# Cutting the last 512 bytes of two cache loads into many small transfers

## The chip, the cores and the metric

The kernel runs on one core of one Trainium2 chip. The core has a matrix engine (TensorE, PE in the profile), a vector engine (VectorE, DVE), a scalar engine (ScalarE, ACT), a general engine (GpSimd, POOL), a queue processor (SyncE, SP) and 16 DMA engines that move data from HBM into the on-chip memory SBUF. The metric is the device time of one execution in microseconds; before the change it is 354.47 us, the median of two executions (354.26 and 354.67).

## The reference, cut to what matters

A decode step for one token of width 512. The large inputs are the two caches: 8 key/value heads, 32768 positions each, 128 numbers of bfloat16 per position, so 8 MiB per head for K and as much for V.

```python
mod = (_silu(c) @ w_mod).reshape(c.shape[0], 6, 1, -1)      # six rows of 512
h = _layernorm(x) * (1 + ca) + sa
q = (h @ wq)                                                # 32 query heads, 4 to a key/value head
scores = einsum('bhqd,bhkd->bhqk', q, k) * Dh ** (-0.5)     # k repeated 4 times
o = einsum('bhqk,bhkd->bhqd', softmax(scores), v)
x = x + ga * (o @ wo)
h = _layernorm(x) * (1 + cb) + sb
x = x + gb * (relu(h @ w1) @ w2)                            # hidden width 1792
```

Every byte of K, V and of the weights is read once and used for a few products only.

## The kernel before, in words

**Tiles.** A head's K (or V) lies in SBUF as 128 partitions with 256 consecutive positions each: 64 KiB in a partition. `kv` and `vv` (L66, L67) are these views of the caches. Three buffers of that size make up the ring (L80); each holds in turn one head's K, one head's V, the pair of `w_mod` and `wq`, or at the end the tail (`wo`, `w1`, `w2`). A new load takes the buffer that was given out three loads earlier, so its transfer is issued only after the work on that earlier content is done.

**Order of loads.** `stream` (L162 to L168) lists the loads by hand: half of K of head 0, `w_mod`, `wq`, the other half of K of head 0, then K of head 1, V of head 0, K of head 2, V of head 1, and so on; the last heads go in halves and quarters, and `wo`, `w1`, `w2` come last. `need` (L171) runs `load` for the next entries of the list until the wanted one is there. `stream_dma` (L153, the transfer itself L154) issues each on SP's queue and stamps it so that the order is kept. A whole head (8 MiB) is one transfer of 128 rows of 64 KiB; a half is 128 rows of 32 KiB. After V of head 0, 14 SP drains follow (L145).

**Completion semaphores.** The framework gives each transfer of SP's and ACT's queues one of eight completion semaphores, in turn. The two small loads of `c` and `A_x` on ACT's queue (L182) take part in the turn. A wait for a transfer is a wait on its semaphore.

**The two loads of the change.** The second half of K of head 0 (the key `UNEVEN`, L57) is cut in `load` (L136 to L141): first all 128 rows without their last 512 bytes (`EDGE`), then the last 512 bytes of rows 0 to 110 (`MOST` is 111), then those of the other 17 rows. V of head 1 is one transfer on SP's queue (L143).

**Compute.** For each head, DVE transposes K in place in eight pieces (L439, 32-bit blocks), PE makes the scores into PSUM (L458), and a softmax over DVE, PE and ACT (L466 to L510) gives the weights, which DVE transposes (L500); PE multiplies them with V (L520) in a loop on PE (L527). Within the loop over heads (L643), K of head g+1 is handled first, then V of head g. K of head 0 is used in quarters: the third transpose and scores of its second half come before the fourth, and only the fourth touches the last 512 bytes. GpSimd does constants in the first 3 us and one memset near the end (L718). After the last head come `wo`, a layer norm, `w1`, `w2` (L784) and the output (L789 to L792).

Of the kernel before, what the change touches and what calls it, by code (L numbers as in the profile page):

```python
# [17 lines left out]
def kernel(  # L18
# [14 lines left out]
    nc = tc.nc  # L33
    P = 128
    _, _, D = A_x.shape
    _, Hkv, Sk, Dh = A_k_cache.shape
# [6 lines left out]
    TK = 64  # L43
# [10 lines left out]

    OUT0, OUT1 = 30, 34

    UNEVEN, EDGE, MOST = ("k", 0, (2, 3)), 2 * TK * Dh - D // 2, 111  # L57
    SPACE = 14
    assert Dh == 128 and REP == 4 and D == 512 and FT == W2P[-1][1] and NTILE == 4
    scale = float(Dh) ** -0.5  # L60
    eps = 1e-5
# [8 lines left out]
    def wo_v(i):  # L70
        g0, n = WOP[i]
        return A_wo[g0 * REP * Dh:(g0 + n) * REP * Dh, :].rearrange("(p r) d -> p r d", p=P)
# [32 lines left out]
    def piece(name, at, n):  # L105

        if name not in pieces:
            pieces[name] = ring.tile([P, NTILE * TK * Dh], BF16, tag="slot", name=name)
        return pieces[name][:, at:at + n]

    def load(key):
        kind = key[0]
        if kind == "wm":
            t = piece("wmq_sb", 0, WM).rearrange("p (kt n) -> p kt n", kt=KT)
            src = wm_v
        elif kind == "wq":
            t = piece("wmq_sb", WM, WQ).rearrange("p (kt n) -> p kt n", kt=KT)
            src = wq_v
        elif kind in "kv":
            g, steps = key[1], key[2]  # L120
            src = (kv if kind == "k" else vv)[g, :, TK * steps[0]:TK * (steps[-1] + 1), :]
            name = f"Ksb{g}" if kind == "k" else f"Vsb{g}"
            t = piece(name, TK * Dh * steps[0], TK * Dh * len(steps)).rearrange("p (j d) -> p j d", d=Dh)
        elif kind == "wo":
            g0, n = WOP[key[1]]
            t = piece("tail_sb", g0 * REP * D, n * REP * D).rearrange("p (r d) -> p r d", d=D)
            src = wo_v(key[1])
        elif kind == "w1":
            k0, k1 = W1P[key[1]]
            t = piece("tail_sb", WO + k0 * Dff, (k1 - k0) * Dff).rearrange("p (kt f) -> p kt f", f=Dff)  # L130
            src = w1_v[:, k0:k1]
        else:
            f0, f1 = W2P[key[1]]
            t = piece("tail_sb", WO + KT * Dff + f0 * D, (f1 - f0) * D).rearrange("p (f d) -> p f d", d=D)
            src = w2_v[:, f0:f1]
        if key == UNEVEN:  # L136
            row, src_row = (x.rearrange("p j d -> p (j d)") for x in (t, src))
            for rows, cols in (
                (slice(0, P), slice(0, EDGE)), (slice(0, MOST), slice(EDGE, None)), (slice(MOST, P), slice(EDGE, None)),
            ):  # L140
                stream_dma(row[rows, cols], src_row[rows, cols])  # L141
        else:
            stream_dma(t, src)  # L143
        if key[:2] == ("v", 0):
            for _ in range(SPACE):  # L145
                nc.sync.drain()
        if kind in "kv":
            for i, u in enumerate(steps):
                loaded[(kind, g, u)] = t[:, TK * i:TK * (i + 1), :]
        else:  # L150
            loaded[key] = t

    def stream_dma(dst, src):  # L153
        i = nc.sync.dma_start(out=dst, in_=src)  # L154
        tc.stamp_issue_order_token(i.ins, "sp_stream")
        if last_loop:

            tc.add_manual_dep(i.ins, last_loop[0], mybir.DependencyInfo(
                mybir.DependencyClass.NoSync, mybir.DependencyReason.DATA))
# [11 lines left out]
    def need(key):  # L171
        while key not in loaded:
            load(stream[pos[0]])
            pos[0] += 1
        return loaded[key]
# [19 lines left out]
    for hp in range(4):  # L195
        h, par = hp // 2, hp % 2
        src = AP(ib.tensor, ib.offset + 64 * h + par, [[ib.ap[0][0], P], [0, 4], [2, 32]])
# [8 lines left out]
        out=mask4, in_=ident_f[:].rearrange("p (x q) -> p q x", q=REP), op=ALU.add, axis=AX.X,  # L206
# [3 lines left out]
    for n in sorted({n * REP for _, n in WOP}):  # L210
        cmask[n] = const.tile([P, P // n], F32, name=f"cmask{n}")
        nc.vector.tensor_reduce(
            out=cmask[n][:], in_=ident_f[:].rearrange("p (c r) -> p c r", r=n), op=ALU.add, axis=AX.X,
# [3 lines left out]
            out=rsel_f[:], in_=ident_f[:].rearrange("p (c r) -> p r c", r=n), op=ALU.add, axis=AX.X,  # L217
# [6 lines left out]
        out=smask[:], in_=ident_f[0:16, 0:16].rearrange("p (s q) -> p s q", q=REP), op=ALU.add, axis=AX.X,  # L224
# [8 lines left out]
        out=place32[:], in_=ident_f[:].rearrange("p (j m) -> p m j", m=32), op=ALU.add, axis=AX.X,  # L233
# [4 lines left out]
        out=rowpick[:, OUT0:OUT1], in_=ident_f[:].rearrange("p (j m) -> p j m", m=32), op=ALU.add, axis=AX.X,  # L238
# [8 lines left out]
        out=cx_bd, in0=cx_row[:].unsqueeze(1).to_broadcast([16, 8, D // 8]),  # L247
# [80 lines left out]
    for u in range(2):  # L328
        for half in range(2):
            t = need(("k", 0, u))[:, 32 * half:32 * half + 32, :].rearrange("p j d -> p (j d)").bitcast(F32)  # L330
# [29 lines left out]
    def four_rows(e, name):  # L360
# [16 lines left out]
        out=nca[:], in0=modT_sb[:, KT:2 * KT], scalar1=-1.0, scalar2=-1.0, op0=ALU.mult, op1=ALU.add,  # L377
# [3 lines left out]
        out=ncb[:], in0=modT_sb[:, 4 * KT:5 * KT], scalar1=-1.0, scalar2=-1.0, op0=ALU.mult, op1=ALU.add,  # L381
# [17 lines left out]
    for i in range(2):  # L399
        nc.vector.transpose(out=q_cols[:, i, :], in_=q_ps[i])  # L400
        nc.scalar.copy(
            out=qT_sb[:, 16 * i:16 * (i + 1)], in_=q_cols[:, i, :].rearrange("p (h r) -> p h r", r=32)[:, :, 0],
# [230 lines left out]
    with tc.manual_schedule(engines={mybir.EngineType.PE, mybir.EngineType.DVE}):  # L633
# [54 lines left out]
        for u in (2, 3):  # L688
# [49 lines left out]
            out=x1T[:], in0=x1T[:], scalar=1.0, in1=xT, op0=ALU.mult, op1=ALU.add, accum_out=stat2[:, 0:1],  # L738
# [31 lines left out]
        for f0, f1 in ((0, FT // 2), (FT // 2, FT)):  # L770
            nc.vector.transpose(out=hidT[:, f0:f1], in_=hid_v[:, f0:f1])
            nc.scalar.activation(
                out=AP(hb.tensor, hb.offset + 32 * f0 + 31, [hb.ap[0], [32, f1 - f0]]),
                in_=hidT[:, f0:f1, 0], func=ACT.Relu,
            )

        for part, (f0, f1) in enumerate(W2P):
            w2_sb = need(("w2", part))
            for ft in range(f0, f1):
                for i in (0, 2, 1, 3):  # L780
                    row = OUT0 + i
                    to, w = (0, 32) if row < 32 else (32, OUT1 - 32)
                    at = 32 * ft + 31 - (row - to)
# [39 lines left out]
```

## Time and profile before

| What | Value |
|---|---|
| Median of two executions | 354.47 us |
| The profiled execution: span from first to last instruction | 352.6 us |
| Bytes read from HBM in it | 149.42 MB, 424 GB/s over the span |
| PE, DVE, ACT, POOL busy | 79%, 57%, 7%, 1% of the span |
| DMA share of SP's queue | 98.5% of 16 engines' span |

The profiled execution has no time of its own on record beside its span. The timed executions are 1.9 us longer than that span at the median; the profile does not say what that difference is made of.

How to read it: the page lists the busy time of each engine, the span in 40 slices, the DMA queues (q1 is SP's, q10 ACT's), the chain of work that ended last and the costliest groups. "Us to landing" of a transfer counts from its issue to the arrival of its last bytes, so it holds the time that it stood in the queue behind earlier ones. In the timeline of SP, a row gives start and duration of an issue, not of the transfer.

### The profile page before, as it was taken

To read this page: it belongs to the slowest core of one execution; us is meant where nothing else is said; L and a number is where in the kernel's file an instruction comes from. 1 tells how busy PE (TensorE), PEld (TensorE's weight loads), DVE (VectorE), ACT (ScalarE), POOL (GpSimd) and SP (SyncE) were. 2 spreads that over 40 slices of the span, in tenths; PEclk is the share of its full clock that TensorE was granted. 3 is DMA by queue.
4 is the path that set the end of the run, shared out by engine and by line. 5 is a ranking of instruction groups with operands and counts; after the bars stand their busy time and mean duration, and the time that the engine had idled before them with its cause. 6 is when DMAs were issued, how large, how long until landed. Compare 5 with 4: busy or idle time off the path is not lost. (4 is left out here: it accounts for less than half of the span.)

```text
span 352.6 us, 3715 instructions
## 1 busy us (share of the span) xinstructions
PE 277.9 (79%) x1310; PEld 113.5 (32%) x1310; DVE 201.0 (57%) x226; ACT 25.1 (7%) x69; POOL 3.1 (1%) x15
## 2 busy tenths in 40 slices
PE   0065891895998599976998499968999799989994
PEld 0021330331333234322333134323444233434442
DVE  6663564984079614974099506975684257744142
ACT  1200103002000200001000200011000100011000
POOL 2000000000000000000000000000000000000000
PEclk9999897798999879998999879996999989999999
DMA  9999989999999999999999999999999999999995
GB/s 357 398 435 452 472 388 461 454 394 454 461 394 448 439 424 439 424 433 439 416 446 446 409 440 461 411 394 454 431 414 435 457 417 420 444 439 409 425 425 214
DMA packets 5224, 149.59 MB, mean 424 GB/s; under 512 B 604, under 2 KB 988, under 8 KB 1628
## 3 DMA queue, kind: packets, MB, share of 16 engines
q1 hardware_dynamic: 5180, 149.43, 98.5%
q8 instruction: 8, 0.13, 0.1%
q14 instruction: 4, 0.03, 0.0%
q10 hardware_dynamic: 32, 0.00, 0.0%
HBM read 149.42 MB, written 0.00 MB: 424 GB/s over the span
## 5 line engine op out<-in xcount | busy, mean ns | idle before, releaser
L439 DVE STREAM_TRANSPOSE Ksb<-Ksb 128x2048 f32<-128x2048 f32 x60 | 133.1, 2276 | 60.2 <-DMA Ksb<-in_A_k_cache_dram 60.2
L520 PE MATMUL o_ps<-Vsb,P_g 128*16 (+1 forms) x512 | 127.0, 408 | 13.0 <-ACT P_g L495 10.0
L458 PE MATMUL S_ps<-Ksb,qbd 128*128 128x512 bf16 x512 | 120.4, 386 | 10.9 <-DVE Ksb L439 9.3
L458 PEld LDWEIGHTS <-qbd 128*128 128x128 bf16 x512 | 49.6, 98 | 78.1 <-issue 21.8
L520 PEld LDWEIGHTS o_ps<-Vsb,P_g 128*16 x352 | 34.0, 97 | 67.8 <-issue 36.5
L520 PEld LDWEIGHTS <-P_g 128*16 128x16 bf16 x160 | 13.8, 90 | 19.0 <-issue 0.4
L420 ACT COPY qbd<-qrep_sb 32x16 bf16<-32x16 bf16 x32 | 6.4, 201 | 175.2 <-PE S_ps L458 174.1
L500 DVE STREAM_TRANSPOSE P_g<-P_g 128x1024 bf16<-128x1024 bf16 x8 | 10.0, 1245 | 14.1 <-ACT P_g L495 14.1
L471 DVE TENSOR_REDUCE m_p<-S_ps 128x1 f32<-128x1024 f32 x7 | 8.6, 1223 | 13.3 <-PE S_ps L458 13.3
L322 PE MATMUL mod_ps<-wmq_sb,siluT 128*1 128x512 bf16 x24 | 3.6, 624 | 9.9 <-DMA wmq_sb<-in_w_mod_dram 9.9
L331 DVE STREAM_TRANSPOSE Ksb<-Ksb 128x2048 f32<-128x2048 f32 x4 | 8.9, 2280 | 1.6 <-DMA Ksb<-in_A_k_cache_dram 1.6
L476 PE MATMUL mT_ps<-ident_f,m_p 128*1 128x128 f32 x8 | 2.2, 270 | 8.9 <-DVE m_p L471 7.9
L495 ACT ACTIVATE P_g<-S_ps,nbias 128x1024 bf16<-128x1024 f32 x8 | 8.9, 1114 | 0.2
L506 PE MATMUL L_ps<-Lexp,ones_f 128*128 128x4 f32 x16 | 3.1, 263 | 6.3 <-DVE Lexp L503 4.3
L492 ACT ACTIVATE nbias<-Mb_ps 128x1 f32<-128x1 f32 x8 | 1.4, 171 | 88.3 <-PE Mb_ps L490 88.3
L509 DVE RECIPROCAL Linv<-L_ps 128x4 f32<-128x4 f32 x8 | 1.3, 164 | 10.9 <-PE L_ps L506 10.9
L252 PE MATMUL xc_ps<-cx_sel,wmq_sb 16*128 16x2 bf16 x4 | 0.3, 172 | 8.7 <-DVE wmq_sb L246 8.7
L555 PE MATMUL acc_ps<-mask_sb,Y 16*128 16x4 f32 x16 | 3.0, 258 | 4.9 <-DVE Y L551 4.9
L548 DVE TENSOR_TENSOR o_ps<-o_ps,smask 16x512 f32<-16x512 f32 x8 | 5.3, 668 | 2.8 <-PE o_ps L520 2.8
L586 DVE CAST o_sb<-o_ps 128x4 bf16<-128x4 f32 (+2 forms) x4 | 0.7, 165 | 10.3 <-PE o_ps L582 10.3
L506 PEld LDWEIGHTS L_ps<-Lexp,ones_f 128*128 128x128 f32 x16 | 2.6, 203 | 9.6 <-issue 5.6
L551 DVE TENSOR_REDUCE Y<-o_ps 16x128 f32<-16x512 f32 x8 | 5.4, 678 | 0.3
(116 smaller groups left out, 82.8 us busy)
## 6 DMA issues: line engine op xcount, KB each, us to landing
Ksb<-in_A_k_cache_dram SPq DMA_DIRECT2D x5, 4096.0 KB, 23.5
Vsb<-in_A_v_cache_dram SPq DMA_DIRECT2D x5, 4096.0 KB, 38.0
wmq_sb<-in_A_wq_dram SPq DMA_DIRECT2D x1, 4096.0 KB, 28.0
Vsb<-in_A_v_cache_dram SPq DMA_DIRECT2D x2, 2048.0 KB, 38.1
Ksb<-in_A_k_cache_dram SPq DMA_DIRECT2D x1, 4032.0 KB, 37.1
wmq_sb<-in_w_mod_dram SPq DMA_DIRECT2D x1, 3072.0 KB, 18.8
tail_sb<-in_A_wo_dram SPq DMA_DIRECT2D x1, 2048.0 KB, 23.0
tail_sb<-in_B_w_dram SPq DMA_DIRECT2D x1, 1792.0 KB, 30.4
```

The lines of the kernel that those rows point to most:

```text
L322: nc.tensor.matmul(dst[j // 4][32 * (j % 4):32 * (j % 4) + 1, :], lhsT=src_T[:, kt:kt + 1], rhs=w[:, kt, j * 512:(j + 1) * 512], start=(kt ...
L331: nc.vector.transpose(out=t, in_=t)
L420: nc.scalar.copy(out=o, in_=i)
L439: t = nc.vector.transpose(out=KTt.bitcast(F32), in_=KTt.bitcast(F32))
L458: nc.tensor.matmul(S_ps_tiles[g], lhsT=qbd[g % 2][:, hp, 4 * (7 - s):4 * (7 - s) + P], rhs=KTv[:, 16 * sl:16 * sl + 16, h, :, par], start= ...
L471: behind_loop(nc.vector.reduce_max(out=m_p[:], in_=S_g.rearrange("p g f -> p (g f)"), axis=AX.X))
L495: nc.scalar.activation(out=P_g[:], in_=S_g.rearrange("p g f -> p (g f)"), func=ACT.Exp, bias=nbias[:], scale=scale, accum_out=l_g[:],)
L500: behind_loop(nc.vector.transpose(out=P_g[:], in_=P_g[:]))
L506: nc.tensor.matmul(L_ps[:], lhsT=ones_f[:], rhs=Lexp[:], start=True, stop=True)
L520: nc.tensor.matmul(o_tiles[g][:], lhsT=PT, rhs=Vx, start=False, stop=False, skip_group_check=True)
L548: nc.vector.tensor_tensor(out=o, in0=o, in1=smask[:].unsqueeze(2).to_broadcast([16, 4, Dh]), op=ALU.mult,)
L551: nc.vector.tensor_reduce(out=Y[:], in_=o.rearrange("p s d -> p d s"), op=ALU.add, axis=AX.X)
```

## The change

Two loads are cut in another way; the bytes and their places in SBUF stay the same.

For the second half of K of head 0, the last 512 bytes of the 128 rows go in 15 transfers in place of two: of 15, 14, 13 and so on down to 2 rows, and one of 9 rows, all on SP's queue behind the transfer of the other columns.

V of head 1 is cut too: SP's transfer leaves out the last 512 bytes of each row, and 16 transfers issued by GpSimd bring these: 14 of 17 rows by 256 bytes, then two of 9 rows by 256 bytes.

```diff
-    UNEVEN, EDGE, MOST = ("k", 0, (2, 3)), 2 * TK * Dh - D // 2, 111
+    UNEVEN, EDGE = ("k", 0, (2, 3)), 2 * TK * Dh - D // 2
     SPACE = 14
+    PROBED = ("v", 1, (0, 1, 2, 3))
...
         if key == UNEVEN:
             row, src_row = (x.rearrange("p j d -> p (j d)") for x in (t, src))
-            for rows, cols in (
-                (slice(0, P), slice(0, EDGE)), (slice(0, MOST), slice(EDGE, None)), (slice(MOST, P), slice(EDGE, None)),
-            ):
-                stream_dma(row[rows, cols], src_row[rows, cols])
+            stream_dma(row[:, 0:EDGE], src_row[:, 0:EDGE])
+            at = 0
+            for n in (15, 14, 13, 12, 11, 10, 9, 8, 7, 6, 5, 4, 3, 2, 9):
+                stream_dma(row[at:at + n, EDGE:], src_row[at:at + n, EDGE:])
+                at += n
+        elif key == PROBED:
+            row, src_row = (x.rearrange("p j d -> p (j d)") for x in (t, src))
+            n = row.shape[1]
+            stream_dma(row[:, 0:n - 256], src_row[:, 0:n - 256])
+            for part in range(7):
+                for c0 in (n - 256, n - 128):
+                    rows, cols = slice(17 * part, 17 * part + 17), slice(c0, c0 + 128)
+                    nc.gpsimd.dma_start(out=row[rows, cols], in_=src_row[rows, cols])
+            for c0 in (n - 256, n - 128):
+                rows, cols = slice(119, P), slice(c0, c0 + 128)
+                nc.gpsimd.dma_start(out=row[rows, cols], in_=src_row[rows, cols])
         else:
             stream_dma(t, src)
```

## The prediction

> **What bounds the kernel now.** I read the page's DMA part first, then the chain.
>
> ```profile
> span 352.6 us, 3715 instructions
> ...
> PE 277.9 (79%) x1310; PEld 113.5 (32%) x1310; DVE 201.0 (57%) x226; ACT 25.1 (7%) x69; POOL 3.1 (1%) x15
> ...
> DMA  9999989999999999999999999999999999999995
> q1 hardware_dynamic: 5180, 149.43, 98.5%
> q8 instruction: 8, 0.13, 0.1%
> HBM read 149.42 MB, written 0.00 MB: 424 GB/s over the span
> ...
> 349.62 0.29 PE end_ps L784 x4
> ```
>
> The reader is to see that the DMA engines are busy in every slice but the last, and that SP's queue alone takes 98.5% of them: 347.3 of 352.6 us, with the rest at the two ends. The last line is from the chain in order of time: the last product runs at 349.62, right behind the last piece of `w2`, and 3.0 us of compute and output end the span. So the time is the length of one unbroken stream of transfers plus fixed ends. A microsecond in which the engines have nothing to move in the middle of the stream is a microsecond of the result; PE (79%) and DVE (57%) cannot take it back. What I look for in the change is therefore whether it makes the stream shorter, or lets it run dry.
>
> **What lets SP issue a transfer.** Next come SP's timeline and the time to landing of single issues, at the end of the kernel, where SP waits for no buffer:
>
> ```profile
> 290.81 0.43 SPq L154 DMA_DIRECT2D Vsb<-in_A_v_cache_dram  x1
> Vsb<-in_A_v_cache_dram SPq DMA_DIRECT2D x1, 2048.0 KB, 40.3
> 313.02 0.33 SPq L154 DMA_DIRECT2D tail_sb<-in_A_wo_dram  x1
> tail_sb<-in_A_wo_dram SPq DMA_DIRECT2D x1, 2048.0 KB, 23.0
> ...
> 331.14 0.33 SPq L154 DMA_DIRECT2D tail_sb<-in_B_w_dram  x1
> 335.99 0.33 SPq L154 DMA_DIRECT2D tail_sb<-in_B_w_dram  x1
> ```
>
> The last quarter of V, issued at 290.81, lands 40.3 us later, at 331.1; the third piece of `w2` is issued at 331.14. The first piece of `wo` lands at 313.02 + 23.0 = 336.0; the fourth piece of `w2` goes at 335.99. Counted in the list of loads, each pair is eight transfers apart (V's last quarter, `wo` four times, `w1`, then `w2` one, two, three). None of these pieces needs the other's data or buffer. They share a semaphore: eight serve all of SP's and ACT's transfers in turn, so **a transfer is issued only when the one eight places before it has landed**. In the old order this never bites ahead of the tail, since few transfers are on their way; I take it as the rule that decides here.
>
> **The change, part by part.** First the K half. The issues at the start, and their landings:
>
> ```profile
> 2.12 0.49 SPq L154 DMA_DIRECT2D Ksb<-in_A_k_cache_dram  x1
> Ksb<-in_A_k_cache_dram SPq DMA_DIRECT2D x1, 4032.0 KB, 37.1
> 8.66 14.46 SPq L154 DMA_DIRECT2D Ksb<-in_A_k_cache_dram  x1
> 313.02 1.75 SPq L154 DMA_DIRECT2D tail_sb<-in_A_wo_dram  x4
> 314.81 0.43 SPq L154 DMA_DIRECT2D tail_sb<-in_B_w_dram  x1
> ```
>
> The large part of the K half is issued at 2.12 and lands at 2.12 + 37.1 = 39.2. In the old kernel two small issues follow, and K of head 1 is handed to the queue from 8.66 to 23.1, long before 39.2: the engines go from one to the other without a pause.
>
> Now 15 small transfers stand between. Number them by rows: the large part, 15, 14, 13, 12, 11, 10, 9 rows fill eight places. The transfer of 8 rows is eight places behind the large part, so SP holds it until 39.2. Behind it in SP's order wait those of 7, 6, 5, 4, 3, 2 and 9 rows and K of head 1, which the engines would need at that very moment; at 39.2 they hold only seven transfers of at most 15 rows. At SP's rate, four issues from 313.02 to 314.81, 0.45 us each, K of head 1 is eight issues after 39.2: 39.2 + 8 x 0.45 = **42.8**. K of head 1 also has to wait for its own forerunner, the transfer of 8 rows, which has had 3.6 us by then; the seven others find theirs long landed. V of head 0 follows at 43.3 and is no problem.
>
> From issue to data there is a start-up, read off the start of the kernel:
>
> ```profile
> 0.74 0.38 SPq L154 DMA_DIRECT2D Ksb<-in_A_k_cache_dram  x1
> Ksb<-in_A_k_cache_dram SPq DMA_DIRECT2D x1, 4096.0 KB, 12.0
> wmq_sb<-in_w_mod_dram SPq DMA_DIRECT2D x1, 3072.0 KB, 18.8
> 1.17 0.43 SPq L154 DMA_DIRECT2D wmq_sb<-in_w_mod_dram  x1
> ...
> 60.18 2.31 DVE L439 STREAM_TRANSPOSE Ksb<-Ksb 128x2048 f32<-128x2048 f32 x1 [0.62 <-DMA Ksb<-in_A_k_cache_dram]
> ```
>
> `w_mod`, queued behind the first K half, lands at 20.0, 7.2 us after that half (12.7) for 3.15 MB: 437 GB/s. At this rate the first half's 4.19 MB are 9.6 us, but 12.0 passed: a start from an empty queue costs 2.4 us, landing included. So K of head 1 (8.39 MB, 19.2 us) lands at 42.8 + 2.4 + 19.2 = 64.4. Unbroken from 39.2 it would land at 58.4: **6.0 us** is the upper end of the loss. In the old kernel it landed only at 60.2, when DVE stops waiting for it: some engines were late there, by the small packets among others. Against that, the loss is **4.2 us**, the lower end, if all of that lateness is gone for good. The lateness at the end of the span has more sources than the first 60 us (instruction loads are on the same engines, 8 packets on q8), so I take most of the upper end: **5.5 us**. The later stream is only shifted: every buffer is freed later by as much as its data came later.
>
> The last 512 bytes of the K half now land with the transfer of 9 rows, issued at 42.3, thus about 44. Only the fourth transpose needs them, and it starts at 39.25 + 3 x 2.2 = 45.9:
>
> ```profile
> 39.25 8.89 DVE L439 STREAM_TRANSPOSE Ksb<-Ksb 128x2048 f32<-128x2048 f32 x4 [3.89 <-DMA Ksb<-in_A_k_cache_dram]
> ```
>
> That is nothing lost, with 2 us of cover; without cover PE's scores of head 0 would wait, on an engine with slack.
>
> What the smaller cuts give the engines: the old 128 rows of 512 bytes sat on few of them.
>
> ```profile
> DMA packets 154, 0.79 MB, mean 524 GB/s; under 512 B 15, under 2 KB 143, under 8 KB 143
> ```
>
> In 38.7 to 40.2 there are 143 - 15 = 128 packets of that size, all of them, so the fullest engine was held for 1.5 us at most; what of that comes back is inside the two ends above. [...]
>
> Then V of head 1. SP's transfer loses 64 KB of 8 MB, under 0.2 us. GpSimd's 16 transfers start when V's buffer is free, as SP's does, and nothing else waits on GpSimd until 313. There is no transfer from GpSimd in the trace. The nearest row is a 1 KB load from ACT's queue beside a full SP queue:
>
> ```profile
> 1.35 0.28 ACTq L182 DMA_DIRECT2D cx_row<-in_A_x_dram  x1
> 7.99 0.68 DVE L246 TENSOR_TENSOR wmq_sb<-cx_row,pick 16x512 bf16<-16x512 bf16 x1 [1.82 <-DMA cx_row<-in_A_x_dram]
> ...
> 79.83 0.33 SPq L154 DMA_DIRECT2D Vsb<-in_A_v_cache_dram  x1
> 123.78 15.57 PE L520 MATMUL o_ps<-Vsb,P_g 128*16 x61 [1.99 <-ACT P_g L495]
> 140.16 0.33 SPq L154 DMA_DIRECT2D Ksb<-in_A_k_cache_dram  x1
> 313.05 0.47 POOL L718 MEMSET tail_sb<- 128x450 bf16 x1 [309.91 <-PE S_ps L458]
> ...
> Vsb<-in_A_v_cache_dram SPq DMA_DIRECT2D x1, 38.2
> 118.48 0.33 SPq L154 DMA_DIRECT2D Vsb<-in_A_v_cache_dram  x1
> ```
>
> It took 6.6 us for one row on each of eight engines, where an engine's 32 KB row is 9.6/8 = 1.2 us: about five rows of the other queue went first. Beside 64 KB rows that is 13 us. If they go eight at a time as on SP's queue, twice over makes 26 us: from 79.8 + 5 to 111, and PE wants V of head 1 at 123.8 + 5. So I price this part at **0**, with nothing below: data that came earlier would gain nothing, since PE waits for ACT's softmax there. If it is late, there is more cover: the next load into this buffer is issued at 140.16, and the queue holds work until V of head 2 lands at 118.48 + 38.2 = 156.7, some 14 us after it counting the start-up.
>
> **Sum:** 5.5 us on a span of 352.6 is 358.1; the timed median, 1.9 us above the span, goes to **360.0**. Two per cent, 7.1 us, is about what a measurement of this kernel can tell from no change, and the forecast lies inside it.
>
> **Rivals.** *The stream does not run dry* (chance 0.08). It needs that SP gets K of head 1 out before 39.2 all the same, because the turn of semaphores runs otherwise than the two pairs above show. Then the old small packets' 1.5 us on the fullest engine is what is left of the change, and a lateness carried to the end is worth all or nothing: 353.0 to 354.5. This is the side of not slower.
>
> *GpSimd's rows come too late* (0.10). If each of its 256-byte rows takes its own turn behind a 64 KB row (2.4 us), 17 rows beside the five turns are 22 turns, 53 us; two rounds are 106 us, V is complete at 191, 62 us after PE wants it, of which 14 are covered: about 48 us more, some 408. With one round, or with several rows to a turn, it is inside the cover. The one-row load does not tell. [...]
>
> *The restart is dearer* (0.10): the first issues after a wait at 0.6 us rather than 0.45, or one engine hit twice by late loads, adds 1.5 to 3.5 us: 361.5 to 363.5, mostly over 2%.
>
> **How the numbers follow.** The forecast has 0.72, from 358.7 (4.2) to 360.5 (6.0), a little wider for the rates. Leaving out the first two rivals (0.18) gives the range 357.5 to 363.5. Slower by over 2%, above 361.6: 0.10 of GpSimd, 0.08 of the dear restart, 0.02 of the forecast's own edge, 0.20. Faster by over 2%: 0.01. Within: 0.79.
>
> **What would show it.** In the changed profile: SP idle ahead of L154 until 39.2, ended by the K half's DMA; eight issues in a row after it; a hole of 4 to 5 us in the DMA busy share from 39.3; K of head 1 landing at 64 in place of 60.2, and every later issue 4 to 6 us later. PE's first product with V of head 1 should wait for ACT, as before, and not for a DMA. It would be wrong if K of head 1 is issued before 39, if the hole is there and the end moves by less than 4 us (an engine that is late anyway), or if GpSimd's transfers land after 129.

## The result, and the profile after

The changed kernel takes 383.08 us (median of two executions, 382.50 and 383.66) against 354.47: the ratio is 1.081, with a 95% interval from 1.0767 to 1.0854. That is 28.6 us slower, far outside the range of 357.5 to 363.5. Single executions of some kernels below, the kernel before among them, are up to 22 us longer than the shortest of the same kernel; the ratios leave out those that are more than 1.5% above the shortest.

The page of the changed kernel, with the lines that answer to those read of before:

```profile
span 381.9 us, 3795 instructions
...
DMA  8999699999999999703999999999999999999991
GB/s 330 439 439 432 228 440 439 439 439 440 432 432 432 420 372 440 330 0 110 434 439 439 432 419 406 414 426 432 439 439 427 432 439 426 414 439 426 418 423 68
...
q1 hardware_dynamic: 5304, 149.36, 91.5%
...
q0 software_dynamic: 512, 0.07, 0.1%
...
HBM read 149.42 MB, written 0.00 MB: 391 GB/s over the span
...
PE 13%; DVE 2%; issue 0%; ACT 0%; ACTq 0%
```

Each slice is 9.5 us wide. The stream now has two holes: a short one in the fifth slice (228 GB/s), which the prediction foresaw, and a deep one from the 17th to the 19th (330, 0 and 110 GB/s), which it did not. SP's queue holds the engines for 91.5% of the span in place of 98.5%. A new queue is there, GpSimd's q0, with 512 packets and next to no bytes. And the chain that ended last is now one of PE. In the kernel before, the same line of the page reads:

```profile
DMA 19%; PE 5%; DVE 3%; SPq 0%; issue 0%
```

The view follows the chain back over the last 60 us or so of the changed kernel, and no DMA is in that part.

SP's timeline shows both holes as late issues:

```profile
2.13 40.17 SPq L167 DMA_DIRECT2D Ksb<-in_A_k_cache_dram  x17
42.42 0.35 SPq L167 DMA_DIRECT2D Vsb<-in_A_v_cache_dram  x1
...
83.98 0.33 SPq L167 DMA_DIRECT2D Vsb<-in_A_v_cache_dram  x1
...
178.82 0.33 SPq L167 DMA_DIRECT2D Ksb<-in_A_k_cache_dram  x1
...
344.55 1.75 SPq L167 DMA_DIRECT2D tail_sb<-in_A_wo_dram  x4
...
379.62 0.29 SPq L805 DMA_DIRECT2D out_dram<-o_bf  x1
```

The first row holds the large part of the K half, the 15 small transfers and K of head 1, and ends at 42.30. V of head 1 goes out at 83.98, 4.15 us later than before (79.83). K of head 4 goes out at 178.82, 38.7 us later (140.16). Then the lateness shrinks: 31.5 us at `wo` (344.55 against 313.02), 29.05 us at the output (before: 350.57).

The two holes by windows, first the changed kernel, then the kernel before; the last two columns are the DMA share and GB/s:

```profile
39.00:44.00 5.00, 5.00 (x21) 2.06 (x20) 4.65 (x3) 0.00 (x0) 0.00 (x0) 0.84 0.62 215
84.00:161.00 77.00, 33.59 (x136) 12.97 (x136) 35.27 (x29) 4.35 (x14) 8.23 (x16) 0.75 0.99 422
161.00:181.00 20.00, 18.11 (x75) 7.28 (x76) 1.61 (x2) 0.00 (x0) 0.00 (x0) 0.85 0.16 52
```

```profile
39.00:44.00 5.00, 5.00 (x23) 2.12 (x22) 4.75 (x3) 0.00 (x0) 0.00 (x0) 0.94 0.99 420
```

From 84 to 161 the stream runs at 422 GB/s, against 424 over the whole span before: GpSimd's transfers hardly slow it here. The hole comes after them, from 161 to 181, with 52 GB/s. What happens in between stands in the timelines of GpSimd and PE and in the time to landing of GpSimd's last transfer:

```profile
84.26 4.16 POOL L151 DMA_DIRECT2D Vsb<-in_A_v_cache_dram  x8 [81.10 <-PE S_ps L471]
93.61 0.51 POOL L151 DMA_DIRECT2D Vsb<-in_A_v_cache_dram  x1 [5.20 <-DMA Vsb<-in_A_v_cache_dram]
98.50 0.51 POOL L151 DMA_DIRECT2D Vsb<-in_A_v_cache_dram  x1 [4.38 <-DMA Vsb<-in_A_v_cache_dram]
103.37 0.51 POOL L151 DMA_DIRECT2D Vsb<-in_A_v_cache_dram  x1 [4.36 <-DMA Vsb<-in_A_v_cache_dram]
105.80 0.51 POOL L151 DMA_DIRECT2D Vsb<-in_A_v_cache_dram  x1 [1.93 <-DMA Vsb<-in_A_v_cache_dram]
...
123.77 0.52 POOL L154 DMA_DIRECT2D Vsb<-in_A_v_cache_dram  x1 [2.07 <-DMA Vsb<-in_A_v_cache_dram]
```

```profile
162.54 16.10 PE L533 MATMUL o_ps<-Vsb,P_g 128*16 x64 [36.23 <-DMA Vsb<-in_A_v_cache_dram]
```

```profile
Vsb<-in_A_v_cache_dram POOLq DMA_DIRECT2D x1, 2.2 KB, 36.9
```

GpSimd issues eight transfers at once and then one each time that an earlier one has landed, mostly some 4.9 us apart (93.61, 98.50, 103.37), now and then half of that (105.80). The last, issued at 123.77, lands 36.9 us later, at 160.7: 76.4 us after the first issue, or 4.8 us for each of 16 on average. PE has waited for it for 36.2 us. Only when PE is done with V of head 1 (162.54 + 16.10 = 178.6) does its buffer come free, and K of head 4 is issued at 178.82. SP's queue had run empty by then.

### The profile page after: what moved, and what is told of

Its sections match the earlier page's. It is cut to its first block, busy times and chain, and to the rows that moved or that the text cites. A ratio compares the mean times of both kernels' runs of the same rounds, so it can differ in the third digit from the quotient of the medians.

```text
span 381.9 us, 3795 instructions
## 1 busy us (share of the span) xinstructions
PE 274.2 (72%) x1310; PEld 112.8 (30%) x1310; DVE 201.0 (53%) x226; ACT 25.1 (7%) x69; POOL 11.3 (3%) x31
## 3 DMA queue, kind: packets, MB, share of 16 engines
q1 hardware_dynamic: 5304, 149.36, 91.5%
## 5 line engine op out<-in xcount | busy, mean ns | idle before, releaser
L533 PE MATMUL o_ps<-Vsb,P_g 128*16 (+1 forms) x512 | 127.0, 407 | 47.2 <-DMA Vsb<-in_A_v_cache_dram 36.2
L471 PE MATMUL S_ps<-Ksb,qbd 128*128 128x512 bf16 x512 | 117.9, 387 | 10.4 <-DVE Ksb L452 9.0
L151 POOL DMA_DIRECT2D Vsb<-in_A_v_cache_dram x14 | 7.2, 522 | 106.5 <-PE S_ps L471 81.1
```

The costliest lines, as they stand in the source:

```text
L151: nc.gpsimd.dma_start(out=row[rows, cols], in_=src_row[rows, cols])
L471: nc.tensor.matmul(S_ps_tiles[g], lhsT=qbd[g % 2][:, hp, 4 * (7 - s):4 * (7 - s) + P], rhs=KTv[:, 16 * sl:16 * sl + 16, h, :, par], start= ...
L533: nc.tensor.matmul(o_tiles[g][:], lhsT=PT, rhs=Vx, start=False, stop=False, skip_group_check=True)
```

## The experiments

All kernels below compute the whole of the reference; only the cut of the transfers differs. The kernel before was timed beside each, with medians from 354.33 to 354.40.

### The K part alone and the V part alone

The K part alone is the changed kernel without its second branch, V of head 1 going as one transfer of SP again.

```diff
-        elif key == PROBED:
-            stream_dma(row[:, 0:n - 256], src_row[:, 0:n - 256])
-            ... 16 x nc.gpsimd.dma_start(...)
```

> The K half cut into the 15 small transfers of the change, V of head 1 in one transfer as before. Theory (the eight semaphores hold back K of head 1 until the large part of the K half has landed): SP issues K of head 1 at about 41.9, as in the changed kernel, the DMA share has a hole of 3 to 4 us from 39, every later issue is about 4.1 us later (in the changed kernel the buffer of V of head 1 came free at 83.98 in place of 79.83), and the time is 354.5 + 4.1 = 358.6, within 357.8 to 360. Rival (all of the loss is in V of head 1, the K cuts are hidden): 354 to 355.

Measured: 359.47 us (359.26 to 359.82), ratio 1.0148 (1.013 to 1.0166). SP's timeline, cut at 39 us, and its later issue of V of head 1:

```profile
39.19 3.04 SPq L155 DMA_DIRECT2D Ksb<-in_A_k_cache_dram  x9
...
83.99 0.33 SPq L155 DMA_DIRECT2D Vsb<-in_A_v_cache_dram  x1
```

Nine issues, the small transfers of 8 down to 2 rows, that of 9 and K of head 1, go within 3.04 us from the landing of the large part on, 0.34 us each. The K part costs 5.1 us, close to the 5.5 of the prediction.

The V part alone keeps the three transfers of the K half as they were:

```diff
+        elif key == PROBED:
+            ... stream_dma(row[:, 0:n - 256], ...) and 16 x nc.gpsimd.dma_start(...)
```

> The K half as before, V of head 1 by SP's transfer and the 16 GpSimd transfers of the change. Theory (the GpSimd transfers pass through all 16 engines one after the other, each two turns behind a 64 KB row of SP's queue, 2 x 2.4 us): the last of them lands 76 us after the first is issued, as in the changed kernel (84.3 to 160.7), thus at 156; PE waits 32 to 36 us for V, the next load into its buffer is issued at about 174 in place of 140.2, and the time is 354.5 + 28.6 - 4.1 = 379, within 377 to 381. Rival (the two parts make each other worse): under 370.

Measured: 378.48 us (two executions), ratio 1.0681 (1.0658 to 1.0704).

```profile
156.68 16.91 PE L532 MATMUL o_ps<-Vsb,P_g 128*16 x64 [34.62 <-DMA Vsb<-in_A_v_cache_dram]
```

PE waits 34.6 us for V of head 1, as in the changed kernel. 24.1 us for the V part and 5.1 for the K part make 29.2, against 28.6 for both: the two add up, and the V part is the large one.

### What sets the pace of GpSimd's transfers

Three reasons could give 76 us: the rows, each with its own turn; a fixed time per transfer; or turns taken per transfer with the other queue. The first kernel of this group brings the same bytes in eight transfers of 16 rows by 512 bytes.

```diff
+            for at in range(0, P, 16):
+                nc.gpsimd.dma_start(out=row[at:at + 16, n - 256:], in_=src_row[at:at + 16, n - 256:])
```

> The K half as before; the last 512 bytes of the rows of V of head 1 by eight GpSimd transfers of 16 rows by 512 bytes in place of 16 by 256 bytes. Same bytes, half as many transfers. Theory (one after the other, two turns of 2.4 us for each): the last lands 5 + 8 x 4.84 = 44 us after the first is issued at 79.8, at about 124, just when PE wants V (123.8); time 354.3 to 355.5. Rival (it is the eight semaphores: the second eight wait for the first eight, and up to eight go side by side): none of these eight waits for another, all have landed 9 to 15 us after the first issue, by 95. The time is the same by both; the landing tells them apart. Third (each row of 512 or 256 bytes has a turn of its own, so rows count and not transfers): 16 rows in a transfer as against 17, and the last lands after about 70 us, at 150, and the time is over 372.

The timeline of its last issue, and its time to landing:

```profile
83.57 0.49 POOL L148 DMA_DIRECT2D Vsb<-in_A_v_cache_dram  x1
```

```profile
Vsb<-in_A_v_cache_dram POOLq DMA_DIRECT2D x1, 8.0 KB, 35.6
```

All eight are out without a wait, from 80.09 to 84.06, and yet the last lands at 119.2 (83.57 + 35.6): 39 us after the first issue, 4.9 us each. So they do not go side by side. My own 124 was too late, since it put 5 us for a start on top of eight times the pace. The time did not settle: four executions from 354.97 to 366.51. That miss is taken up further below.

The next kernel has 12 transfers, of 11 rows by 512 bytes. It has the same 128 rows as the one with eight, so it parts rows from transfers.

```diff
+            for at in range(0, P, 11):
+                nc.gpsimd.dma_start(out=row[at:min(at + 11, P), n - 256:], in_=src_row[at:min(at + 11, P), n - 256:])
```

> The K half as before; the last 512 bytes of the rows of V of head 1 by twelve GpSimd transfers (eleven of 11 rows and one of 7, 512 bytes each) in place of 16. Theory (4.84 us for each, one after the other, and a cover of about 14 us): the last lands 12 x 4.84 = 58 us after the first issue, at 138; PE waits for it about 14 us, the next load into its buffer is issued at about 155 in place of 140, just as the queue runs out, and the time is 354.5 to 357.5. Rival (the loss grows evenly with the number of transfers, 24 us for 16): 18 us, 372.

Its page has this row for GpSimd's queue, and its last transfer, issued at 102.68, this time to landing:

```profile
q0 software_dynamic: 384, 0.07, 0.1%
```

```profile
Vsb<-in_A_v_cache_dram POOLq DMA_DIRECT2D x1, 3.5 KB, 36.0
```

The last lands at 138.7, 57.7 us after the first issue at 80.95: 12 times 4.8. Packets: 512 for 16 transfers, 384 for 12 and, on the page of the kernel with eight, 256: always 32 per transfer, whatever its rows. The packet records of the changed kernel show those of a transfer of 17 rows as eight of 512 bytes, one of 260, seven of eight bytes and 16 of four; the two transfers of 9 rows together have 18 of 256 bytes and 46 of four. By the semaphore records each of the 16 ends with 16 posts to its semaphore. No record names an engine; I read the 32 packets as two on each of the 16 engines, one with data (or a few bytes) and one of four bytes. For the first transfer of the changed kernel the 16 data packets start at 89.5 to 90.4, the 16 of four bytes at 92.0 to 92.8, and the data packets of the second at 94.5 to 95.4: some 2.5 us, about one 64 KiB row of SP, lie between one packet and the next.

The third kernel keeps the 16 transfers of the change and halves the rows of SP's queue beside them: K of heads 2 and 3 and V of heads 1 and 2 go in two transfers of 32 KiB rows each.

```diff
+    SPLIT = [("k", 2, (0, 1, 2, 3)), ("k", 3, (0, 1, 2, 3)), ("v", 2, (0, 1, 2, 3))]
...
+            for c0, c1 in ((0, n // 2), (n // 2, n - 256)):
+                stream_dma(row[:, c0:c1], src_row[:, c0:c1])
...
+        elif key in SPLIT:
+            for j0 in (0, 2 * TK):
+                stream_dma(t[:, j0:j0 + 2 * TK, :], src[:, j0:j0 + 2 * TK, :])
```

> As v_only with its 16 GpSimd transfers, but SP's loads of K of heads 2 and 3 and of V of heads 1 and 2 go as two transfers of 32 KB rows in place of one of 64 KB rows, so that the rows of the other queue are half as long while the GpSimd transfers are under way. Theory (a turn lasts as long as one row of SP's queue): the last GpSimd transfer lands about 5 + 16 x 2.42 = 44 us after the first issue, at 122 to 126, and the time is 354.3 to 356. Rival (each GpSimd transfer has a fixed latency of 4.8 us, made of issue, completion and semaphore, whatever the other queue moves): it lands at 156 as in v_only and the time is 377 to 381.

GpSimd's timeline, and the time to landing of its last transfer, issued at 101.76:

```profile
90.80 0.51 POOL L152 DMA_DIRECT2D Vsb<-in_A_v_cache_dram  x1 [0.70 <-DMA Vsb<-in_A_v_cache_dram]
93.23 0.51 POOL L152 DMA_DIRECT2D Vsb<-in_A_v_cache_dram  x1 [1.92 <-DMA Vsb<-in_A_v_cache_dram]
95.66 0.51 POOL L152 DMA_DIRECT2D Vsb<-in_A_v_cache_dram  x1 [1.92 <-DMA Vsb<-in_A_v_cache_dram]
```

```profile
Vsb<-in_A_v_cache_dram POOLq DMA_DIRECT2D x1, 2.2 KB, 18.0
```

The issues are now mostly 2.43 us apart in place of 4.9, and the last lands at 119.8, 39.5 us after the first issue at 80.25: about half of 76. The same transfers, the same bytes, half the time: a fixed time per transfer is out. A 64 KiB row takes an engine 2.42 us, the median in the packet records of the kernel before, and a transfer of GpSimd takes two of these, one for each packet. The kernel takes 355.21 us (median of ten, two of them 360.1), ratio 1.0054 (1.0014 to 1.0094): with the landing ahead of PE's need for V (123.78 before), the V part costs next to nothing.

### How much lateness the kernel covers

Back to the kernel with 12 transfers. I had expected 354.5 to 357.5, because a landing at 138.7 lay inside the cover that the prediction counts. It measured 361.31 us (360.88 to 362.59), ratio 1.0201 (1.0181 to 1.0221). The landing was right and the time was not. PE's and SP's timelines of it:

```profile
140.92 16.02 PE L527 MATMUL o_ps<-Vsb,P_g 128*16 x64 [18.57 <-issue]
```

```profile
157.11 0.33 SPq L161 DMA_DIRECT2D Ksb<-in_A_k_cache_dram  x1
...
357.50 0.29 SPq L799 DMA_DIRECT2D out_dram<-o_bf  x1
```

PE waits 18.6 us in place of 2.0, K of head 4 is issued 17.0 us late, and the output is still 6.9 us late. Its chain, too, is led by PE and has no DMA in the last 60 us. The last large packet of the stream ends at 352.5, 5.0 us ahead of the output's issue, where it is 2.0 before (348.6 and 350.57). So at the end it is compute that is late, not the stream. How fast compute makes it up stands in SP's issues of one and the same load, K of head 7, in the kernel before:

```profile
256.12 0.33 SPq L154 DMA_DIRECT2D Ksb<-in_A_k_cache_dram  x1
```

Three heads lie between this and 140.16, 38.65 us each; there the stream sets the pace. In the changed kernel K of head 4 goes at 178.82 and the first half of K of head 7 at 288.01, as the same view of it has it: 36.4 us each, and there compute does: from 197 to 297 its DVE waits for transfers of K for 6.7 us in all, against 27.1 us before, 37 us earlier (160 to 260). The kernel gains 2.3 us per head, no more.

If that is so, the same transfers at V of head 4 leave fewer heads in which to make it up:

```diff
-    PROBED = ("v", 1, (0, 1, 2, 3))
+    PROBED = ("v", 4, (0, 1, 2, 3))
```

> The K half as before; the 16 GpSimd transfers of the change moved from V of head 1 to V of head 4, three heads later. They start at 195.9; beside 64 KB rows until 232 they take 4.84 us each, beside the 32 KB rows that follow 2.42 us, so the last lands at about 255, and PE, which wants V of head 4 at 239.7, waits about 16 us, nearly as in v_twelve (18.6). The next load into the buffer is K of head 7, issued at 256 in place before; the queue holds work until 281, so no hole. Theory (compute has only some 2.3 us for each head to make up lateness, by v_twelve: 17.0 late at the load after V of head 1, 9.9 three heads later, 6.9 at the end): with one head left nearly all of it stays, 11 to 14 us, and the time is 363 to 368 with no hole in the DMA share. Rival (only a hole in the stream costs): 354.3 to 356.

Measured: 366.40 us (366.05 to 366.43), ratio 1.034 (1.0324 to 1.0356), inside what was expected. PE's wait, SP's two issues behind it, and a window:

```profile
254.58 16.03 PE L532 MATMUL o_ps<-Vsb,P_g 128*16 x64 [16.64 <-DMA Ksb<-in_A_k_cache_dram]
```

```profile
270.78 0.33 SPq L166 DMA_DIRECT2D Ksb<-in_A_k_cache_dram  x1
285.28 0.33 SPq L166 DMA_DIRECT2D Vsb<-in_A_v_cache_dram  x1
```

```profile
280.00:292.00 12.00, 12.00 (x58) 5.00 (x55) 2.89 (x5) 0.00 (x0) 0.00 (x0) 1.00 0.68 270
```

The view names a K transfer as the releaser; I read it as GpSimd's last, issued at 234.44, which landed after 18.3 us, at 252.7: PE starts 1.9 us after that landing, as in the changed kernel (160.7 and 162.54). (Only 18.3: K and V of head 5 go in halves with 32 KiB rows, so this case confirms the pace once more.) PE is 14.7 us late (K of head 7 at 270.78 against 256.12), and with one head and a half left the end is 12.0 us late. With 12 transfers at V of head 1, a lateness of 17.0 came down to 6.9. That there would be no hole was wrong: from 280 to 292 the engines are busy 68% of the time, some 4 us lost, because V of head 6 was issued only at 285.28.

### Where the eight-place rule begins

The next two kernels cut the edge of the K half in six and in seven transfers. With six, K of head 1 is eight places behind the second half's forerunner `w_q`; with seven it is eight behind the large part.

```diff
-            for n in (15, 14, 13, 12, 11, 10, 9, 8, 7, 6, 5, 4, 3, 2, 9):
+            for n in (22, 22, 21, 21, 21, 21):
```

> The last 512 bytes of the K half in six small transfers (22, 22, 21, 21, 21, 21 rows) behind the large part; V of head 1 as before. K of head 1 is then seven places behind the large part and eight behind w_q's load. Theory (eight semaphores in turn): K of head 1 is issued when that load has landed, at about 29.8, ten microseconds before the K half lands; no hole; the time is 354.4, within 353.6 to 355.2. Rival (many small transfers cost the stream by themselves, some 0.3 us for each of the 15): 354.4 + 6 x 0.33 = 356.4.

```diff
-            for n in (15, 14, 13, 12, 11, 10, 9, 8, 7, 6, 5, 4, 3, 2, 9):
+            for n in (19, 19, 18, 18, 18, 18, 18):
```

> One small transfer more than in k_six (19, 19, 18, 18, 18, 18, 18 rows); V of head 1 as before. K of head 1 is now eight places behind the large part. Theory: it is issued only when the large part has landed, at 39.3 to 39.4, with nothing of size in the queue; the hole is one issue and start, and K of head 1 comes about 2.6 us earlier than in k_only, where it is issued at 41.9 to 42.0: the time is 359.5 - 2.6 = 356.9, within 356 to 357.8, a step of 2 to 3 us against k_six for one transfer more. Rival (a cost for each small transfer): 0.3 us above k_six.

SP's timeline with six, and with seven; the first row of each ends with the issue of K of head 1:

```profile
2.12 27.93 SPq L155 DMA_DIRECT2D Ksb<-in_A_k_cache_dram  x8
...
79.94 0.33 SPq L155 DMA_DIRECT2D Vsb<-in_A_v_cache_dram  x1
```

```profile
2.12 37.54 SPq L155 DMA_DIRECT2D Ksb<-in_A_k_cache_dram  x9
...
81.30 0.33 SPq L155 DMA_DIRECT2D Vsb<-in_A_v_cache_dram  x1
```

With six, K of head 1 is out at 30.05 and the kernel takes 354.85 us, ratio 1.0013 (1.0003 to 1.0022). With seven, it is out at 39.66, behind the landing of the large part, and the kernel takes 357.01 us, ratio 1.0071 (1.0058 to 1.0085). One transfer more makes a step of 2.2 us, at the place where the rule puts it.

The last of this group takes all cuts away: the K half goes in one transfer.

```diff
-        if key == UNEVEN:
-            ... three stream_dma(...)
-        else:
-            stream_dma(t, src)
+        stream_dma(t, src)
```

> The K half in one transfer, no small ones; V of head 1 as before. It gives the price of the two small transfers of the old kernel, whose 128 packets hold some engines up to 1.5 us longer at 39 to 40. Theory (that lateness is not what sets the end; other engines are as late by then): 354.0 to 354.6, no change that shows. Rival (it is carried to the end): 353.0 to 353.6.

Measured: 355.22 us (354.87 to 355.75), ratio 1.0025 (1.0015 to 1.0035), 0.84 us slower than before, where I had expected the same or a little less. So taking away the old small packets' time on a few engines (in the trace of before their two transfers end with three posts to a semaphore and one) shortened nothing. Where the 0.84 come from the runs do not settle; most lies behind the output's issue, which is 0.15 us later than before (350.72 against 350.57).

### A slow stretch of the stream

The two harmless halves together, six transfers for K and eight for V, should have cost about nothing:

```diff
+            for n in (22, 22, 21, 21, 21, 21):
...
+            for at in range(0, P, 16):
```

> Both parts of the change, each with fewer transfers: the last 512 bytes of the K half in six small transfers as in k_six, those of V of head 1 in eight GpSimd transfers of 16 rows by 512 bytes as in v_eight. Theory (six is below the eight semaphores; eight GpSimd transfers take 39 us and end before PE wants V): no hole, no wait of PE for V, 354.8 to 355.6. Rival (the cutting itself costs, whatever the number): nearer to the changed kernel, over 357.

Measured: 361.18 us (359.70 to 361.46), ratio 1.0178 (1.0159 to 1.0197): a miss by 6 us. PE does not wait for V there: its product starts at 124.38, behind 1.99 us of waiting for ACT, as before. I ran the kernel with eight transfers once more, and one in which SP brings the same 512 bytes of V in a second transfer of its own, so that the rows of the first are as long as with GpSimd:

> The same kernel as v_eight, whose four times lay between 354.97 and 366.51. In its profiled execution the rows of all engines took 2.7 us and more for a while after 112 us, which also one execution of the kernel before showed (367.45), so that it looks like a disturbance from outside. If so: most executions at 354.8 to 355.4. If the eight transfers do it: again most over 358.

```diff
+            stream_dma(row[:, 0:n - 256], src_row[:, 0:n - 256])
+            stream_dma(row[:, n - 256:], src_row[:, n - 256:])
```

> The K half as before; V of head 1 by two transfers of SP's queue, the rows without their last 512 bytes and then these 512 bytes of all 128 rows, with none from GpSimd. It asks why v_eight and k_six_v_eight, which make PE wait for nothing, still take some 355 in some executions and 360 in others: in the long ones the rows of all engines take 2.7 to 2.8 us in place of 2.42 from about 114 to 156. If the rows of 65,024 bytes in place of 65,536 bring that about: long executions (over 358) here too, at least a third of them. If it is the GpSimd transfers beside the queue: all executions at 354.2 to 355.2, save one in ten as in the kernel before.

The same window in four kernels: before; six and eight together; eight alone (its first run); and SP alone.

```profile
116.00:152.00 36.00, 29.97 (x126) 12.04 (x124) 20.13 (x19) 2.18 (x7) 0.00 (x0) 0.91 0.99 430
```

```profile
116.00:152.00 36.00, 28.31 (x112) 11.17 (x110) 16.16 (x17) 2.18 (x7) 0.00 (x0) 0.86 1.00 379
```

```profile
116.00:152.00 36.00, 28.37 (x107) 11.02 (x106) 16.58 (x17) 2.18 (x7) 0.00 (x0) 0.81 1.01 379
```

```profile
116.00:152.00 36.00, 29.77 (x125) 11.71 (x124) 20.12 (x19) 2.18 (x7) 0.00 (x0) 0.95 1.01 435
```

In the two with eight transfers of GpSimd the engines are busy all the time (1.00, 1.01) but move 379 GB/s in place of 430. Over 36 us that is 4.3 us of the 6.8 lost. In the packet records of eight alone every 64 KiB row that starts from 120 to 150 takes 2.78 to 2.79 us, before 2.42 to 2.47, so all engines are slower alike; at the 379 GB/s of the window 16 such rows, one for each engine, take 2.77 us. Eight alone, run again, gave twelve executions from 354.89 to 376.30 us, about half of them near 355; ratio 1.0042 (1.0012 to 1.0071). Its profiled execution, of 358.70 us, moves 397 GB/s in this window. With SP alone it is 435 GB/s and 355.11 us (354.86 to 355.41, eleven executions), ratio 1.0019 (1.001 to 1.0028).

The kernel with 12 transfers has such a stretch too, somewhat later; this window of it, and then of the kernel before:

```profile
132.00:158.00 26.00, 16.73 (x69) 6.57 (x70) 9.21 (x6) 0.00 (x0) 0.00 (x0) 0.76 0.97 378
```

```profile
132.00:158.00 26.00, 23.25 (x104) 9.42 (x101) 18.54 (x10) 0.78 (x4) 0.00 (x0) 1.00 1.01 437
```

Its end is set by compute all the same, as shown above, so this does not touch the reading of the cover.

So the shorter rows of SP alone did not bring the stretch about, and it was seen only beside GpSimd's transfers, in some executions. That they cause it is likely but not shown: there is only one profile of the kernel before, and three of its 17 executions timed beside the twelve took 362 to 371 us themselves, none of the 14 beside SP alone. (Of the kernel before's execution of 367.45 us, which the expectation above likens to it, only the time is on record.) Why the engines go at this pace, after the transfers have landed too, stays open.

No kernel here beats the one before.

## Why the prediction was wrong, point by point

**The eight places: right.** "a transfer is issued only when the one eight places before it has landed": K of head 1 left SP behind the large part's landing, and six against seven transfers show the step. In the trace of the changed kernel SP's and ACT's transfers post to eight semaphores in turn, and the small transfers of 12, 10, 9 and 8 rows are issued at 12.82, 20.07, 29.74 and 39.35, each within 0.02 us of the landing of the transfer eight places before (12.80, 20.05, 29.73 and 39.33).

**The price of the K part: right, 5.1 us for 5.5.** Two terms were off and cancelled. SP's issues took 0.34 us each, not 0.45, so K of head 1 was issued at 41.9 (39.2 + 8 x 0.34) in place of 42.8. From there to its landing passed 22.4 us, not 21.6. DVE's timeline of the changed kernel has the landing:

```profile
39.35 8.89 DVE L452 STREAM_TRANSPOSE Ksb<-Ksb 128x2048 f32<-128x2048 f32 x4 [3.76 <-DMA Ksb<-in_A_k_cache_dram]
...
64.33 6.70 DVE L452 STREAM_TRANSPOSE Ksb<-Ksb 128x2048 f32<-128x2048 f32 x3 [4.42 <-DMA Ksb<-in_A_k_cache_dram]
```

DVE's wait for K of head 1 ends at 64.33, where the prediction has 64.4. The first row shows the four transposes unbroken in 8.89 us, as long as before: that the fourth has cover was right. The choice of 5.5 between 4.2 and 6.0 rested on no row, and that it came so near is partly luck: with the K part alone V of head 1 is issued 4.2 us later than before, `wo` 4.7 us (317.68 against 313.02). That the gain from the smaller cuts stays small was right as well; with no cuts at all there was none.

**The V part: wrong, 24.1 us for 0.** The step that failed is "If they go eight at a time as on SP's queue, twice over makes 26 us". Eight in flight was right as a count of issues (84.26, x8) and wrong as a count of transfers that move at once. GpSimd's transfers stand behind each other in one queue, by my reading of the packets on all 16 engines, and each takes two turns there, with a 64 KiB row of SP (2.42 us) before each: 16 x 2 x 2.4 = 77 us, where 76.4 were measured. That the two agree so closely is partly luck: by the semaphore records the first transfer landed only 9.1 us after its issue, and three of the 15 steps from one landing to the next took 2.4 to 2.6 us, the others 4.7 to 5.8. The nearest row that I had was a single transfer, and one transfer cannot show whether several go side by side.

The packets are what the prediction did not add up: 32 for each transfer, those of 9 rows included, are 512 in one queue. It had no transfer from GpSimd to count them on, and its 26 us was my estimate from the one-row load.

**The cover: wrong too.** "Some 14 us" was counted for the stream: SP's queue holds work for so long. But PE stands still meanwhile, and what it loses compute makes up at 2.3 us per head. With 12 transfers SP's queue did not run empty behind the late transfer (DMA share 0.97 to 1.01 in the windows from 116 to 300) and the kernel still lost 6.9 us. In the changed kernel the lateness of 38.7 us at K of head 4 ends as 29.05.

**The rivals.** "GpSimd's rows come too late" had the sign, the waiting product and the landing behind 129. Its unit was wrong: a turn per transfer's packet, not per row, so 76 us in place of 106, and 383.1 us in place of some 408. The forecast of 360.0 fell by the sign that the prediction itself named, "if GpSimd's transfers land after 129": the last landed at 160.7. That the stream does not run dry was refuted by the hole at 39 us, and the dearer restart by the 5.1 us.

**The chances.** The gap between 26 and 106 us in the price of the V part spanned the whole verdict, and one row of a single transfer stood for it. A chance of 0.10 for the upper end was too low for that.

## What to carry to other kernels

Here a small transfer from GpSimd beside SP's full queue paid one row of that queue (2.42 us) for each of its two packets on an engine, so its time was counted in transfers and in the length of the other queue's rows, not in bytes: 4.8 to 4.9 us for 4 KB as for 8 KB. Many of them in one queue added up, even when all were issued at once (39 us for eight); fewer of them (57.7 us for 12 against 76.4 for 16), or shorter rows in the queue beside them (39.5 us for 16), shortened the whole. And before an idle stretch is called cover, ask how fast the engines behind it could make up a delay: a stream that keeps running hides little when compute needs 36.4 of every 38.65 us.

## What the runs showed of the hardware that was not expected

- GpSimd's transfers put 32 packets each on the engines (512, 384 and 256 for 16, 12 and eight transfers), and the time between them halves with the rows of the queue beside them (4.9 and 2.43 us between most issues).
- Late in a run of eight or 12 such transfers and after it the stream ran at 378 to 397 GB/s in place of 430 to 437 for some 26 to 36 us, with the engines busy throughout; with SP's transfers alone this was not seen. The cause is open.
- The K half in one transfer was 0.84 us slower than with its last 512 bytes cut off (355.22 against 354.38). The cause is open.
